# Fetching the next expert's weights in parts, one to two batches ahead, with their quarter sums one at a time between accumulating transfers

## The chip, the cores and the metric

The kernel runs on one core of a Trainium2 chip. The metric is device time in microseconds (us), lower is better. A kernel is run several times, beside runs of the kernel before on the same chip. A ratio is the mean time of one kernel's fast runs over that of the other's fast runs of the same rounds, so it is not quite the ratio of the medians that are quoted. PE is TensorE, ACT is ScalarE, DVE is VectorE, and POOL is GpSimd, which also issues most of this kernel's DMA (76.8 of 94.33 MB, worked out from the issues on the page of before).

## The reference, cut to what matters

Attention with a hash mask produces 3072 tokens of 512 numbers. They then pass through eight experts, each of them two matrices with a ReLU between, weighted by a routing matrix `P`:

```python
B, H, S, D = 4, 8, 768, 64            # 3072 tokens in 4 batches of 768
for e in range(8):
    h = np.maximum(x @ w1[e], 0.0)    # 512 x 1024
    ye = h @ w2[e]                    # 1024 x 512
    out += P[:, e:e + 1] * ye
```

Experts 1 to 7, four batches each, take about two thirds of the time.

## The kernel before

Each product of experts 1 to 7 is computed from 2 x 2 blocks with seven block products instead of eight. This needs sums and differences of the blocks of both operands. The four sums of each weight matrix ("quarter sums") are made on POOL. The four sums of the hidden activations h are made on DVE for each of the three steps of a batch:

```python
wpool = ctx.enter_context(tc.tile_pool(name="wpool", bufs=2))
...
def quarters_of_w(e):
    if (e, 1) not in weights:
        load_w(e, 1, pin=True)              # one 1 MB transfer (f32 to f16), issued by POOL
    ...
    pin(nc.gpsimd.tensor_tensor(s[:, 0], a21, a22, op=Alu.add))
    pin(nc.gpsimd.tensor_tensor(a21, a11, a21, op=Alu.subtract))
    pin(nc.gpsimd.tensor_tensor(s[:, 1], s[:, 0], a11, op=Alu.subtract))
    pin(nc.gpsimd.tensor_tensor(s[:, 2], a12, s[:, 1], op=Alu.subtract))
    ...
# quarters_of_w2(e) does the same for w2

def sums_of_h(e, b, i):                     # on DVE, both inputs in SBUF
    ...
    pin(nc.vector.tensor_tensor(s_[:, 0], h21, h22, op=Alu.add))             # s1
    pin(nc.vector.tensor_tensor(s_[:, 1], s_[:, 0], h11, op=Alu.subtract))   # s2
    pin(nc.vector.tensor_tensor(h21, h11, h21, op=Alu.subtract))             # s3
    pin(nc.vector.tensor_tensor(s_[:, 2], h12, s_[:, 1], op=Alu.subtract))   # s4
```

`pin` keeps an instruction in program order. `hidden(e, b)` makes the h of a batch. `mixed(e, b)` multiplies it by w2 in three steps i = 0, 1, 2. PE alternates between `hidden` of one batch and `mixed` of the batch before it (`woven`). In every step ACT copies four partial results from PSUM into a buffer `vt`, and POOL issues a transfer that adds `vt` to the result `acc`:

```python
def mixed(e, b):
    for i in range(J // 2):
        ...
        vt = vkeep.tile([P, 4, DD // 2], F32, tag="v", name="vt")      # vkeep: bufs=3
        ...                                                            # seven products; ACT fills vt
            if g == 3 and i + 1 < J // 2:
                sums_of_h(e, b, i + 1)
            if g == 6:
                if not last:
                    pin(nc.gpsimd.dma_start(out=acc[:, b, i], in_=vt, accum_op=Alu.add))
...
ORDERS = (("a1", "d", "a2", "y", "a3", "a4", "t"), ...)    # step 0: a2 reads s2, y reads s3, a4 reads s4
...
hspool = ctx.enter_context(tc.tile_pool(name="hspool", bufs=3))
vkeep = ctx.enter_context(tc.tile_pool(name="vkeep", bufs=3))
...
def hidden(e, b):
    if b == 2 and e < E - 1:
        quarters_of_w(e + 1)
    if b == 3 and e < E - 1:
        quarters_of_w2(e + 1)
...
def woven(n):
    h = hidden(*work[n]) ...
    c = mixed(*work[n - 1]) ...
        sums_of_h(*work[n - 1], 0)          # the first DVE sums of a batch: right at its start
```

The softmax here doesn't subtract the row's maximum and nothing guards it: scores larger than these inputs give would overflow.

## Time and profile before

Before takes 915.38 us (median of 3 runs, 914.61 to 917.09).

| expert stage of the kernel before | us | where it is read |
|---|---|---|
| one undisturbed batch | 18.46 | spacing of the accumulating transfers at the end of the run |
| four undisturbed batches | 73.9 | worked out: 4 x 18.46 |
| from expert to expert, mean | 89.3 | spacing of the first weight load of each |
| POOL waits for weights | 127.3 | view of waits: 66.6 + 60.7 |
| ACT waits for a free vt | 66.5 | view of waits |

First a stretch without weight work, from the table of windows. Its columns are start and end, length, then busy time and number of instructions of PE, PE's weight loads, DVE, ACT and POOL, then PE's granted clock, the DMA share, and GB/s. PE is busy for 64.49 of 65.00 us at full clock, so PE is the bound wherever nothing stops it.

```profile
800.00:865.00 65.00, 64.49 (x490) 47.63 (x489) 49.64 (x116) 41.55 (x97) 9.29 (x11) 1.00 0.57 117
```

The view of waits has who waited for whom, then us in total, times, and the longest. These are the lines of the loop that stops PE:

```profile
POOL t L147 <- DMA t<-in_moe_w_dram: 66.6, 5, 13.6
ACT vt L208 <- DMA acc<-vt: 66.5, 12, 7.2
...
PE a L201 <- ACT vt L208: 62.4, 17, 6.4
...
POOL s L134 <- DMA t<-in_moe_w_dram: 60.7, 6, 10.6
```

POOL's timeline around one such place follows (start, duration, line, operation; in brackets the idle time before it and what ended it). The load goes out at 558.00, POOL sits for 10.60 us, then runs four sums of about 2.1 us. The accumulating transfers that came due meanwhile go out three in a row (x3) at 578.30. The same happens for w2 until 604.75 (this one wait, of 14.27 us, the view puts down to PE; the other five of L147 it puts down to the load).

```profile
557.47 0.84 POOL L246 DMA_DIRECT2D acc<-vt  x1 [4.60 <-ACT hT L664]
558.00 1.09 POOL L113 DMA_DIRECT2D t<-in_moe_w_dram  x1
569.70 2.12 POOL L134 TENSOR_TENSOR s<-t 128x1024 f16<-128x1024 f16 x1 [10.60 <-DMA t<-in_moe_w_dram]
...
578.30 2.57 POOL L246 DMA_DIRECT2D acc<-vt  x3
579.97 1.84 POOL L113 DMA_DIRECT2D t<-in_moe_w_dram  x1
596.08 2.12 POOL L147 TENSOR_TENSOR t<-t 128x1024 f16<-128x1024 f16 x1 [14.27 <-PE y L201]
...
604.75 2.62 POOL L246 DMA_DIRECT2D acc<-vt  x3
```

PE's timeline at the same place: it stops for 6.40 us, because ACT has no free vt, and then the four matmuls of a group take 1.01 us in place of 0.60. The windows view gives a granted clock of 0.52 from 583.8 to 588.6.

```profile
575.69 0.60 PE L201 MATMUL a<-t,hT 128*128 128x256 f16 x4
...
583.80 1.01 PE L201 MATMUL a<-t,hs 128*128 128x256 f16 x4 [6.40 <-ACT vt L208]
```

POOL sums also meet the DVE sums of h (L176 to L179, usually 0.42 us each) in this trace: 17 of the DVE sums last 0.77 to 2.38 us. Eleven fall within 2 us before one of the stalls on vt, where a delay can't be told from the stall. Two of the rest are shown. At 506 us the last DVE sum, s4, is held up, and PE loses 0.23 us. At 774 us three POOL sums in a row hold up three DVE sums, s2, s3 and s4, and PE loses 4.10 us. What PE waits for last, both times, is the DVE operation L215 (it adds a product to `acc`), which comes after them:

```profile
506.00 0.42 DVE L178 TENSOR_TENSOR hT<-hT 128x512 f16<-128x512 f16 x1
506.02 2.38 POOL L147 TENSOR_TENSOR t<-t 128x1024 f16<-128x1024 f16 x1 [13.20 <-DMA t<-in_moe_w_dram]
506.33 2.35 DVE L179 TENSOR_TENSOR hs<-hT,hs 128x512 f16<-128x512 f16 x1
...
509.99 0.60 PE L201 MATMUL y<-t,hT 128*128 128x256 f16 x4 [0.23 <-DVE acc L215]
...
774.74 2.12 POOL L147 TENSOR_TENSOR t<-t 128x1024 f16<-128x1024 f16 x1 [13.32 <-DMA t<-in_moe_w_dram]
774.76 2.38 DVE L177 TENSOR_TENSOR hs<-hs,hT 128x512 f16<-128x512 f16 x1
...
777.06 2.34 DVE L178 TENSOR_TENSOR hT<-hT 128x512 f16<-128x512 f16 x1
...
779.32 2.33 DVE L179 TENSOR_TENSOR hs<-hT,hs 128x512 f16<-128x512 f16 x1
...
782.96 1.00 PE L201 MATMUL y<-t,hT 128*128 128x256 f16 x4 [4.10 <-DVE acc L215]
```

### The profile page before, as it was taken

What the parts mean: (1) busy time and instruction counts of PE and PEld (TensorE: products, weight loads), DVE (VectorE), ACT (ScalarE), POOL (GpSimd) and SP (SyncE); (2) the same over time, 40 slices, a digit from 0 to 9 for tenths busy, and PEclk for the clock granted to TensorE, in tenths of its full rate; (3) what the DMA queues carried; (4) which work ended last, traced back from release to release, by engine and by line L of the source; (5) the groups of instructions that cost most, each with busy time, mean ns of one, the idle gap of its engine ahead of it and who ended that gap; (6) DMA issues with size and microseconds to landing.
All of it is one profiled execution on the core that took longest, in us unless ns stands there. A gap on an engine that the chain in (4) does not pass through costs nothing.

```text
span 916.0 us, 16844 instructions
## 1 busy us (share of the span) xinstructions
PE 781.9 (85%) x6412; PEld 536.5 (59%) x6412; DVE 560.0 (61%) x1213; ACT 516.7 (56%) x1033; POOL 300.0 (33%) x311
## 2 busy tenths in 40 slices
PE   4789999998999789978997899779977997899830
PEld 1456666565556557755775577457755775577620
DVE  2335656454658766766775677557765776777710
ACT  1767677776457567644664466446644664466510
POOL 6545443491001541154115412441244134311110
PEclk9879999999999899989998999889998998999965
DMA  6965576410004555555366445634564456447653
GB/s 190 243 155 155 139 182 131 127 40 1 1 1 86 92 94 99 102 92 102 74 116 105 80 92 93 115 70 92 93 116 82 81 93 116 93 79 149 141 119 89
DMA packets 44720, 94.33 MB, mean 103 GB/s; under 512 B 10656, under 2 KB 23968, under 8 KB 44640
## 3 DMA queue, kind: packets, MB, share of 16 engines
q0 software_dynamic: 29920, 77.88, 44.5%
q1 hardware_dynamic: 13920, 14.77, 5.9%
q8 instruction: 50, 0.82, 0.4%
q10 hardware_dynamic: 800, 0.62, 0.3%
q14 instruction: 30, 0.25, 0.1%
HBM read 53.14 MB, written 7.08 MB: 66 GB/s over the span
## 4 chain that ended last, share of the span: by engine, by line
PE 52%; DMA 23%; POOL 7%; issue 6%; ACT 5%; DVE 4%; SPq 1%; POOLq 0%; ACTq 0%; DVEq 0%
PE a L201 10%; PE a L625 10%; DMA t<-in_moe_w_dram 9%; DMA acc<-vt 8%; PE d L625 7%; PE y L201 5%; PE st L418 5%; PE hp L476 3%; PE num L434 2%; PE yp L159 2%; ACT pt L421 2%; PE yp L486 2%; PE d L201 2%; POOL t L135 1%; POOL s L136 1%
## 5 line engine op out<-in xcount | busy, mean ns | idle before, releaser
L208 ACT ACTIVATE vt<-a,p 128x256 f32<-128x256 f32 x335 | 158.5, 473 | 233.5 <-PE a L201 167.0
L634 DVE CUSTOM_DVE_ANT_0 hT<-d,u 128x384 f16<-128x384 f32 x336 | 185.1, 553 | 168.9 <-ACT u L630 163.8
L201 PE MATMUL a<-t,hs 128*128 128x256 f16 x1008 | 162.3, 287 | 63.5 <-ACT vt L208 62.4
L421 ACT ACTIVATE pt<-st 128x768 f16<-128x768 f32 x192 | 147.2, 809 | 72.9 <-PE st L418 72.1
L246 POOL DMA_DIRECT2D acc<-vt x83 | 71.0, 972 | 333.6 <-ACT vt L208 119.9
L630 ACT COPY u<-a 128x384 f32<-128x384 f32 x336 | 160.7, 478 | 32.7 <-PE a L625 24.2
L201 PEld LDWEIGHTS <-hT 128*128 128x128 f16 x1344 | 134.1, 100 | 61.1 <-issue 9.6
L201 PEld LDWEIGHTS <-hs 128*128 128x128 f16 x1008 | 102.7, 102 | 107.5 <-issue 58.0
L625 PE MATMUL a<-xT,s 128*128 128x384 f16 x448 | 116.4, 343 | 0.1
L418 PE MATMUL st<-qs,ks 71*128 71x384 f16 x384 | 98.1, 338 | 17.4 <-DMA qs<-ds 13.2
L625 PEld LDWEIGHTS <-t 128*128 128x128 f16 x896 | 89.2, 100 | 39.4 <-issue 4.8
L201 PE MATMUL y<-t,hT 128*128 128x256 f16 x672 | 106.6, 284 | 5.1 <-DVE acc L215 5.0
L625 PE MATMUL d<-xd,t 128*128 128x384 f16 x448 | 109.8, 327 | 0.0
L215 DVE SCALAR_TENSOR_TENSOR acc<-y,p,acc 128x256 f32<-128x256 f32 x168 | 80.3, 478 | 17.2 <-PE y L201 17.1
L434 PEld LDWEIGHTS <-pt 128*128 128x128 f16 x1152 | 62.5, 99 | 28.5 <-issue 3.9
L625 PEld LDWEIGHTS <-s 128*128 128x128 f16 x672 | 67.8, 101 | 19.4 <-issue 2.3
L434 PE MATMUL num<-va,pt 128*128 128x65 f16 x1152 | 68.4, 196 | 0.6 <-ACT pt L421 0.6
L625 PE MATMUL a<-xT,t 128*128 128x384 f16 x224 | 57.2, 338 | 0.0
L625 PE MATMUL d<-xT,t 128*128 128x384 f16 x224 | 56.3, 334 | 0.0
L330 POOL CAST t<-acc 128x768 f16<-128x768 f32 x32 | 26.3, 825 | 90.6 <-DVE acc L329 90.3
L418 PEld LDWEIGHTS <-ks 71*128 71x128 f16 x384 | 33.4, 100 | 38.5 <-issue 13.1
L664 ACT ACTIVATE hT<-a 128x384 f16<-128x384 f32 x112 | 54.1, 483 | 2.9 <-PE a L625 2.9
(94 smaller groups left out, 961.8 us busy)
## 6 DMA issues: line engine op xcount, KB each, us to landing
acc<-vt POOLq DMA_DIRECT2D x83, 512.0 KB, 5.1
t<-in_moe_w_dram POOLq DMA_DIRECT2D x16, 1024.0 KB, 11.2
acc<-in_k_dram POOLq DMA_DIRECT2D x7, 768.0 KB, 5.7
acc<-in_q_dram POOLq DMA_DIRECT2D x7, 768.0 KB, 6.0
v<-in_v_dram POOLq DMA_DIRECT2D x28, 192.0 KB, 4.5
out_dram<-acc SPq DMA_DIRECT2D x18, 256.0 KB
ks<-t SPq DMA_DIRECT2D x64, 48.0 KB
qs<-t SPq DMA_DIRECT2D x56, 48.0 KB
```

The source lines that it names most:

```text
L201: pin(nc.tensor.matmul(dst, hq[hn][:, fo, :], wq[wn][:, fo, :], start=first and fo == 0, stop=fo == FH - 1, skip_group_check=True))
L208: pin(nc.scalar.activation(out=vt[:, k], in_=a, func=Act.Copy, scale=p))
L215: pin(nc.vector.scalar_tensor_tensor(out=dst, in0=src, scalar=p, in1=dst, op0=Alu.mult, op1=Alu.add))
L246: pin(nc.gpsimd.dma_start(out=acc[:, b, i], in_=vt, accum_op=Alu.add))
L418: pin(nc.tensor.matmul(st[:, i, 0:HT], d["k"][0:KR, h, kt * P:(kt + 1) * P], d["q"][0:KR, h, i * HT:(i + 1) * HT], start=True, stop=True))
L421: pin(nc.scalar.activation(out=pt, in_=st[:, :, 0:HT], func=Act.Exp, scale=scale))
L434: pin(nc.tensor.matmul(num[:, j * (D + 1):(j + 1) * (D + 1)], pf[:, j * P:(j + 1) * P], va[:, h, kt, :], start=(kt == 0 and j == 0), stop= ...
L476: pin(nc.tensor.matmul(hp[:, 0:HT], w1[:, do, fo * P:(fo + 1) * P], xT[:, do, b * S + t * HT:b * S + (t + 1) * HT], start=(do == 0), stop= ...
L625: pin(nc.tensor.matmul(bk, wq[wn][:, do, f * P:(f + 1) * P], xq[xn][:, do, :], start=first and do == 0, stop=do == 1, skip_group_check=True))
L630: pin(nc.scalar.copy(t, bk))
L634: pin(add(TENSOR_ADD_SAT, out=dst, in0=bk, in1=u, s0=3e38, s1=0.0))
L664: pin(nc.scalar.activation(out=hT[:, f, hi], in_=a, func=Act.Relu))
```

## The change

The intent is that POOL should never sit waiting for weights. Loads are cut into halves and issued well ahead. At the end of every step (`next(coming)`, after the accumulating transfer) POOL gets one half load or one quarter sum, or nothing. There are three steps per batch, so twelve such places ("slots") per expert. Slots 1, 2, 4 and 5 load. Slots 6 to 13 sum, where 13 is also slot 1 of the expert after and gets a sum and a load. Slots 6, 9 and 12 are ends of batches. One hs buffer is given up and one vt buffer is added.

```diff
-    def load_w(e, which, pin=False):
+    def load_w(e, which, pin=False, half=None):
...
+        part = slice(0, t.shape[1]) if half is None else slice(half * t.shape[1] // 2, (half + 1) * t.shape[1] // 2)
+        ins = nc.gpsimd.dma_start(out=t[:, part], in_=src[:, part])
...
         pin(nc.gpsimd.tensor_tensor(s[:, 0], a21, a22, op=Alu.add))
+        yield
         pin(nc.gpsimd.tensor_tensor(a21, a11, a21, op=Alu.subtract))
+        yield
...                                          # likewise after the other sums, and in quarters_of_w2
+    def next_weights():
+        for e in range(2, E):
+            for which in (1, 2):
+                for half in range(2):
+                    load_w(e, which, pin=True, half=half)
+                    yield
+                if which == 1:
+                    yield
+            for g in (quarters_of_w(e), quarters_of_w2(e)):
+                for n in range(4):
+                    next(g, None)
+                    if g.__name__ == "quarters_of_w" or n < 3:
+                        yield
+        while True:
+            yield
+    coming = next_weights()
...                                          # mixed, end of each step, after the accumulating transfer
+                    next(coming)
...
-    hspool = ctx.enter_context(tc.tile_pool(name="hspool", bufs=3))
-    vkeep = ctx.enter_context(tc.tile_pool(name="vkeep", bufs=3))
+    hspool = ctx.enter_context(tc.tile_pool(name="hspool", bufs=2))
+    vkeep = ctx.enter_context(tc.tile_pool(name="vkeep", bufs=4))
...                                          # hidden
-        if b == 2 and e < E - 1:
-            quarters_of_w(e + 1)
-        if b == 3 and e < E - 1:
-            quarters_of_w2(e + 1)
...                                          # woven
+        if n == 0:
+            for _ in range(3):
+                next(coming)
```

More of the change, by code (lines that the diff above doesn't have):

```diff
@@ L104 @@
     weights = {}
-    def load_w(e, which, pin=False):
-        if which == 1:
+    def load_w(e, which, pin=False, half=None):
+        if half == 1:
+            t = weights[e, which]
+            src = (moe_w1[e].rearrange("(do di) f -> di do f", di=P) if which == 1
+                   else moe_w2[e].rearrange("(fo fi) d -> fi fo d", fi=P))
+        elif which == 1:
             t = wpool.tile([P, DO, F], F16, tag="w1")
@@ L112, in load_w @@
             src = moe_w2[e].rearrange("(fo fi) d -> fi fo d", fi=P)
-        ins = nc.gpsimd.dma_start(out=t, in_=src)
+        part = slice(0, t.shape[1]) if half is None else slice(half * t.shape[1] // 2, (half + 1) * t.shape[1] // 2)
+        ins = nc.gpsimd.dma_start(out=t[:, part], in_=src[:, part])
         if pin:
@@ L147, in quarters_of_w2 @@
         pin(nc.gpsimd.tensor_tensor(t[:, 1], b22, b12, op=Alu.subtract))
+        yield
         pin(nc.gpsimd.tensor_tensor(b12, b12, b11, op=Alu.subtract))
+        yield
         pin(nc.gpsimd.tensor_tensor(t[:, 0], b22, b12, op=Alu.subtract))
+        yield
         pin(nc.gpsimd.tensor_tensor(t[:, 2], b21, t[:, 0], op=Alu.subtract))
         weights[e, "t"] = dict(b11=b11, t1=b12, b21=b21, b22=b22, t2=t[:, 0], t3=t[:, 1], t4=t[:, 2])
+    def next_weights():
[3 more added lines that the diff above has]
+                    load_w(e, which, pin=True, half=half)
+                    yield
+                if which == 1:
+                    yield
+            for g in (quarters_of_w(e), quarters_of_w2(e)):
+                for n in range(4):
+                    next(g, None)
+                    if g.__name__ == "quarters_of_w" or n < 3:
+                        yield
+        while True:
+            yield
+    coming = next_weights()
     def combine(b):
@@ L525 @@
             if n == len(groups) - 1 and i == 2:
-                quarters_of_w(1)
-                quarters_of_w2(1)
+                for _ in quarters_of_w(1):
+                    pass
+                for _ in quarters_of_w2(1):
+                    pass
             if u + 1 < len(units):
```

## The prediction

Three passages that rest on no trace of this case are cut from the recorded text where marked. Its sum came to 915.4 - 93 + 5 = 827 us. The 93 is worked out from the trace of before, the 5 is an estimate from the two meetings in it.

> **What bounds the kernel now.** After about 260 us the expert stage is bound by TensorE: undisturbed, PE is busy 64.5 of 65.0 us (table of windows, 800 to 865 us, clock 1.00), and one batch takes 18.46 us (every third accumulating transfer in the timeline of POOL). Four batches are 73.9 us, but experts follow each other every 88.4 to 91.7 us, 89.3 on average (first weight load of each). So 15.4 us per expert is lost, some 93 us over six transitions.
>
> **Where it goes.** POOL's timeline shows one queue doing all: it issues a whole 1 MB weight load, sits 10 to 14 us until it lands (view of waits: 66.6 us for w2, 60.7 us for w1), then runs four sums of 2.12 us. The accumulating transfers acc<-vt due meanwhile stand behind this; three go out together afterwards (578.30, 604.75). With three vt buffers ScalarE then waits for one (66.5 us, 12 times), and TensorE for ScalarE: twelve stalls of 4.0 to 6.4 us, 62 us together, two per expert. After each the matmul groups last 1.01 us in place of 0.60 for some 4.5 us, about 2.3 us more per stall, 27 us together. [...] gaps of 0.5 us leave 0.60. 62 + 27 = 89 us, close to 93.
>
> **What the change does.** Same bytes, same eight sums. Loads go out in halves at the ends of steps, at least four steps (about 24 us) before the first sum that reads them, so POOL should never sit on one. Between two accumulating transfers stands at most one sum (2.1 us) or one half load's issue (about 1 us), with 6.15 us from step to step. A fourth vt buffer gives a transfer about 18 us to land; alone it takes 5.1, and behind a half load (estimated 5.6, half of the whole's 11.2) some 11. The third hs buffer isn't needed: its last reader is a step old when it is rewritten.
>
> **New cost.** The sums now run beside full-speed compute. The DVE sums of h (two SBUF inputs, 0.42 us) sometimes take 2.27 us beside a POOL sum[...]. Three of eight sums per expert fall at a batch's end, where the next DVE sums are due. In the trace such a collision cost TensorE 0.23 us, once 4.1 us. I allow 0.2 to 0.5 us for each of some 20 collisions: 4 to 10 us. Attention, routing and the 51 us tail stay.
>
> **Predicted:** 915.4 - 93 + 5 = 827 us; 816 to 845 should hold it 8 times in 10. Faster by over 2%: 0.96; within 2%: 0.03; slower: 0.01.
>
> **What would show it.** POOL's waits for weight loads vanish; ScalarE's wait for acc<-vt falls from 66.5 us to under 5; no 1.01 us matmul groups between 265 and 860 us; experts every 74 to 76 us. DVE sums of over 2 us grow in number, with PE waits under 1 us on DVE. Landing of acc<-vt rises (maximum about 12 us) but nobody waits.
>
> **What would make it wrong.** Collisions might idle TensorE long enough to drop its clock; two half loads in succession might delay acc<-vt beyond four buffers[...]. Each would leave it at 840 to 870.

## The result, and the profile after

The changed kernel takes 869.96 us (median of 4 runs, 868.53 to 874.65) against 916.24 us (4 runs, 914.61 to 918.03). The ratio of the fast runs is 0.9503, with a 95% interval of 0.946 to 0.9547. That is 5% faster, but above the predicted range of 816 to 845.

In the view of waits the loop of before is gone. POOL waits for no weight load any more, and ACT waits for no accumulating transfer. A new pair stands in its place: PE, and PE's weight loads, wait 18 times for the DVE sum on L207, which is s2 (17 of them, of 1.6 to 2.4 us, at the end of a batch whose slot has a sum; the last is 0.5 us at the end of the run).

```profile
PEld L231 <- DVE hs L207: 39.8, 18, 2.8
...
PE a L231 <- DVE hs L207: 33.1, 18, 2.4
```

POOL's timeline shows the plan at work: single loads and single sums between the transfers, with no waiting for weights. From 594.83 to 613.28, with no sum at the batch's end, a batch takes 18.45 us, as long as an undisturbed one of before.

```profile
588.44 0.85 POOL L276 DMA_DIRECT2D acc<-vt  x1 [5.71 <-ACT vt L238]
589.04 2.40 POOL L161 TENSOR_TENSOR t<-t 128x1024 f16<-128x1024 f16 x1
591.12 1.01 POOL L118 DMA_DIRECT2D t<-in_moe_w_dram  x1
594.83 0.86 POOL L276 DMA_DIRECT2D acc<-vt  x1 [2.71 <-ACT hT L693]
...
613.28 0.83 POOL L276 DMA_DIRECT2D acc<-vt  x1 [4.49 <-ACT hT L693]
...
619.32 2.41 POOL L139 TENSOR_TENSOR s<-t 128x1024 f16<-128x1024 f16 x1
```

The next batch, with the sum at 619.32 at its end, has its second transfers at 613.28 and 633.82 us: 20.54 us. So a sum at a batch's end costs 2.1 us. The timeline of all engines at such a place shows how. The transfer goes out at 559.21, just as the DVE sums of the next batch begin. The POOL sum follows at 559.81 and ends at 562.20. The DVE sum s2, started at 559.50, lasts 2.99 us instead of 0.42 and ends at 562.49. The first PE product that reads s2 starts then, after 1.89 us of idling.

```profile
559.05 0.42 DVE L206 TENSOR_TENSOR hs<-hT 128x512 f16<-128x512 f16 x1
559.21 0.85 POOL L276 DMA_DIRECT2D acc<-vt  x1 [2.43 <-ACT hT L693]
...
559.50 2.99 DVE L207 TENSOR_TENSOR hs<-hs,hT 128x512 f16<-128x512 f16 x1
...
559.81 2.39 POOL L145 TENSOR_TENSOR s<-t,s 128x1024 f16<-128x1024 f16 x1
...
562.42 0.41 DVE L208 TENSOR_TENSOR hT<-hT 128x512 f16<-128x512 f16 x1
...
562.55 0.61 PE L231 MATMUL a<-t,hs 128*128 128x256 f16 x4 [1.89 <-DVE hs L207]
```

The account runs over the same 26 batches in both traces, from the first accumulating transfer of all to the first one of the second-last batch. Before needs 851.4 - 278.8 = 572.6 us and after 805.8 - 280.1 = 525.7 us. Undisturbed they would need 484.0: 3 batches of the first expert at 19.8 us (the spacing of its matmul groups in the trace of before, 278.29 to 298.08) and 23 of 18.46. So before lost 88.6 us there and after loses 41.7 us. The old stalls are gone, and nearly half of their worth was given back to the new wait.

### The profile page after: what moved, and what is told of

It is laid out like the page before. It is cut to its first block, busy times and chain, and to the rows that moved or that the text cites. A ratio compares the mean times of both kernels' runs of the same rounds, so it can differ in the third digit from the quotient of the medians.

```text
span 866.8 us, 16857 instructions
## 1 busy us (share of the span) xinstructions
PE 763.8 (88%) x6412; PEld 526.9 (61%) x6412; DVE 583.7 (67%) x1213; ACT 514.9 (59%) x1033; POOL 308.0 (36%) x323
## 4 chain that ended last, share of the span: by engine, by line
PE 68%; DVE 13%; ACT 7%; DMA 5%; issue 2%; POOL 1%; SPq 0%; ACTq 0%; POOLq 0%
PE a L231 14%; PE a L654 14%; PE d L654 9%; PE y L231 7%; PE st L449 6%; DVE hs L207 6%; ACT pt L452 4%; DVE hT L663 4%; PE hp L507 4%; PE num L465 3%; DMA acc<-vt 3%; PE yp L517 2%; PE yp L189 2%; PE d L231 2%; DVE acc L245 2%
## 5 line engine op out<-in xcount | busy, mean ns | idle before, releaser
L231 PE MATMUL a<-t,hs 128*128 128x256 f16 x1008 | 153.2, 275 | 35.9 <-DVE hs L207 33.1
L231 PEld LDWEIGHTS <-hT 128*128 128x128 f16 x1344 | 131.3, 98 | 53.8 <-issue 2.0
L231 PEld LDWEIGHTS <-hs 128*128 128x128 f16 x1008 | 97.8, 99 | 78.1 <-DVE hs L207 39.8
L654 PE MATMUL a<-xT,s 128*128 128x384 f16 x448 | 111.2, 330 | 0.1
L231 PE MATMUL y<-t,hT 128*128 128x256 f16 x672 | 101.8, 274 | 1.7 <-DVE hT L208 1.1
L207 DVE TENSOR_TENSOR hs<-hs,hT 128x512 f16<-128x512 f16 x84 | 79.4, 946 | 2.9
L654 PEld LDWEIGHTS <-s 128*128 128x128 f16 x672 | 66.0, 98 | 17.8 <-issue 2.3
L654 PE MATMUL a<-xT,t 128*128 128x384 f16 x224 | 55.2, 328 | 0.0
```

The costliest lines, as they stand in the source:

```text
L231: pin(nc.tensor.matmul(dst, hq[hn][:, fo, :], wq[wn][:, fo, :], start=first and fo == 0, stop=fo == FH - 1, skip_group_check=True))
L654: pin(nc.tensor.matmul(bk, wq[wn][:, do, f * P:(f + 1) * P], xq[xn][:, do, :], start=first and do == 0, stop=do == 1, skip_group_check=True))
```

## The experiments

The theory after the result: the 42 us are lost where a POOL sum runs at the same time as the first DVE sums of a batch. Four rivals were tested. The first is that a POOL sum costs its time wherever it stands. The second is that a batch's end is dear for another reason. The third is that each meeting has a fixed price. The fourth is that half loads or late transfers cause the loss. A separate question is which part of the change earned the gain.

For most of the experiments the generator was replaced by one with two tables, so that only a table differs from run to run:

```python
LOADS = {1: (1, 0), 2: (1, 1), 4: (2, 0), 5: (2, 1)}     # slot: (matrix, half), as in the change
SUMS = {6: 1, 7: 1, 8: 1, 9: 1, 10: 1, 11: 1, 12: 1, 13: 1}   # slot: number of sums, as in the change

def next_weights():
    todo = {e: eight_sums(e) for e in range(2, E)}        # the sums of w1, then of w2, one per next()
    slot = 0
    while True:
        slot += 1
        for e in range(2, E):
            for _ in range(SUMS.get(slot - 12 * (e - 2), 0)):
                next(todo[e])
        for e in range(2, E):
            if slot - 12 * (e - 2) in LOADS:
                which, half = LOADS[slot - 12 * (e - 2)]
                load_w(e, which, pin=True, half=half)
        yield
```

| run | what it is | median us | ratio to before (95%) |
|---|---|---|---|
| the change | | 869.96 | 0.9503 (0.946 to 0.9547) |
| a1_off_ends | no sum at a batch's end | 836.35 | 0.9118 (0.9073 to 0.9163) |
| f1_no_sums | no sums at all for experts 2 to 7 (wrong result) | 831.65 | 0.907 (0.9014 to 0.9127) |
| c1_before_4vt | before, with the change's buffers only | 872.31 | 0.9515 (0.947 to 0.956) |
| d1_after_3vt | the change, with before's buffers | 868.89 | 0.9434 (0.9359 to 0.9509) |
| g1_pause | the change, batch-end sums about 1.5 us later | 838.52 | 0.9153 (0.9109 to 0.9197) |
| h1_half_sums | half a sum at a batch's end | 849.9 | 0.927 (0.9221 to 0.9319) |
| i1_off_ends_3vt | a1 with before's buffers | 830.89 | 0.9075 (0.9023 to 0.9127) |
| j1_off_ends_whole | a1 with whole loads | 834.31 | 0.9107 (0.9062 to 0.9152) |
| b2_early_only | early whole loads, sums in fours at batch ends, before's buffers | 902.1 | 0.9835 (0.9756 to 0.9915) |

All are medians of four runs and gave correct results, except f1. Its output is wrong, which doesn't matter for the time. The runs were made on three chips, each beside its own runs of before, so they are compared by their ratios. One run of d1, the profiled one, fell in the slow state. Its ratio uses the other three (858.47 to 869.0), and its trace is not used.

### Sums moved off the ends of batches (a1_off_ends)

```diff
-    SUMS = {6: 1, 7: 1, 8: 1, 9: 1, 10: 1, 11: 1, 12: 1, 13: 1}
+    SUMS = {4: 1, 5: 1, 7: 1, 8: 1, 10: 1, 11: 1, 13: 1, 14: 1}
```

> Same loads, same eight sums, but one sum at the end of the first and of the second step of a batch and none at a batch's end. Theory (the lost time sits where a POOL sum meets the first DVE sums of the next batch): the 18 TensorE waits of about 1.9 us for the DVE sum s2 vanish, a batch takes 18.46 us throughout, 828 to 834 us. Rival (a POOL sum costs about 2 us of DVE time wherever it stands): no better than 865 us.

Measured: 836.35 us. The same eight sums and the same loads, moved by a step or so, take about 34 us less. No s2 sum in the trace is longer than 0.43 us (the line below is from the view of tile hs; after the count come the least, median and greatest duration in ns, then the first and last start). Of the waits of PE for it, one of 0.5 us is left at the end of the run.

```profile
L213 DVE TENSOR_TENSOR hs<-hs,hT x84: 424/425/426, 270.9 to 785.3; 128x512 f16<-128x512 f16 x84
```

So a sum does not cost its time wherever it stands, and the first rival falls. The result is 2 us above the expected range. In the trace PE still waits 1.37 and 1.28 us for the DVE in the first expert, where DVE also makes the block sums of x. Four of these take 2.65 to 2.94 us beside a POOL sum, where the others take 0.55.

### No sums at all (f1_no_sums)

```diff
         s = spool.tile([P, 3, 2, F // 2], F16, tag="s1")
+        (for e > 1: raw quarters take the place of the sums, no POOL operation; the same for w2)
```

> The changed kernel with the sums of experts 2 to 7 taken away (raw quarters in their place: wrong result on purpose). Theory: the same as without sums at batch ends, 826 to 832 us, since the other sums cost nothing. Rival (something else, such as the half loads or the landing of transfers, makes the 2 us): stays at 860 us or more.

Measured: 831.65 us, with half loads and transfers as in the change. Its interval overlaps those of a1 and i1, so sums away from the ends of batches cost nothing that these times can tell from noise. The traces tell a little more. By the account over 26 batches a1 still loses 767.2 - 279.0 - 484.0 = 4.3 us, most of it in the first expert, and f1 loses 0.4, against the 41.7 of the change. The half loads and the landing of transfers do not make the 42 us, and the fourth rival falls.

### Only the buffers (c1_before_4vt), and all but the buffers (d1_after_3vt)

```diff
 c1: before, with          hspool bufs=3 -> 2, vkeep bufs=3 -> 4
 d1: the change, with      hspool bufs=2 -> 3, vkeep bufs=4 -> 3
```

> The kernel before with only the buffers of the change: vt 4, hs 2. A stall of 4.0 to 6.4 us ends when one more transfer has landed, and a fourth buffer gives 5.4 to 6.6 us more. If the buffer is the larger part of the gain, 840 to 870 us. If the early fetch and spreading are what counts, 900 us or more.

> The changed kernel with the buffers of before: vt 3, hs 3. With POOL never blocked a transfer has 12 us to land. If early fetch and spreading are what counts, 868 to 876 us. If the fourth buffer is, 890 us or more with ScalarE waiting for acc<-vt behind the half loads.

Measured: 872.31 us, 2 us above the range that was expected if the buffer counts, and 868.89 us, in the range expected if the early fetch does. I had not seen this coming when I predicted: one more vt buffer alone, with POOL still sitting on whole loads, earns what the whole change earns. The rescheduling alone, without the buffer, earns it as well. The two are substitutes. That each removes the stall on vt is seen in the trace of c1; for d1 it is inferred, from its time and from i1 below, which has the same three buffers. In c1's view of waits POOL still waits for the weights, but ACT hardly waits for transfers. PE now waits for the DVE sums here as well, because the eight POOL sums, no longer hidden in a stall, run beside them (at 491 to 497 us DVE sums of 1.57, 2.22 and 2.33 us beside POOL sums of 2.12 to 2.18):

```profile
POOL s L134 <- DMA t<-in_moe_w_dram: 60.4, 6, 10.6
...
PE a L201 <- DVE hs L177: 19.1, 12, 3.0
...
PE y L201 <- DVE hT L178: 6.3, 6, 1.3
ACT vt L208 <- DMA acc<-vt: 5.4, 5, 1.5
```

### The batch-end sum a little later (g1_pause)

```diff
+                    if slot % 3 == 0:                                 # a batch's end
+                        pin(nc.gpsimd.memset(pauses[0], 0.0))         # 128 x 640 f16
+                        pin(nc.gpsimd.memset(pauses[0], 0.0))
                     next(todo[e])
```

> The changed kernel's order of sums; only each of the 18 batch-end sums stands behind two write-only fills on POOL (about 1.25 us, estimated from the 0.195 us of a 128-wide and 1.39 us of a 1560-wide fill). Theory (what costs is the overlap in time with the four DVE sums of h, which last some 1.7 us): the sum starts when they are over, and 18 x 2.07 us come back: 830 to 842 us, s2 at 0.42 us. Rival (a sum at a batch end is dear for another reason, e.g. it holds up the transfer behind it): 868 us or more, as POOL has more to do.

Measured: 838.52 us, though POOL has more to do. The sum stands at the same slot, behind the same transfer and in the same order, but starts 2.1 us after that transfer instead of 0.6. The DVE sums are over by then. Thus a batch's end is dear only for the overlap in time, and the second rival falls. The trace also shows that the fills, which only write, run beside the DVE sums (L218 to L220) without lengthening them. A DVE sum that meets the POOL sum, the next step's at 523.90, is lengthened to 0.87 us, but has time to spare.

```profile
520.50 0.43 DVE L218 TENSOR_TENSOR hs<-hs,hT 128x512 f16<-128x512 f16 x1
520.76 0.94 POOL L183 MEMSET pause<- 128x640 f16 x1
520.84 0.42 DVE L219 TENSOR_TENSOR hT<-hT 128x512 f16<-128x512 f16 x1
521.18 0.42 DVE L220 TENSOR_TENSOR hs<-hT,hs 128x512 f16<-128x512 f16 x1
...
522.36 2.13 POOL L139 TENSOR_TENSOR s<-t 128x1024 f16<-128x1024 f16 x1
523.90 0.87 DVE L217 TENSOR_TENSOR hs<-hT 128x512 f16<-128x512 f16 x1
```

### Half a sum at the batch's end (h1_half_sums)

```diff
-        pin(nc.gpsimd.tensor_tensor(s[:, 0], a21, a22, op=Alu.add))
+        hsum(s[:, 0], a21, a22, Alu.add, 0)      # first half of the columns
+        yield
+        hsum(s[:, 0], a21, a22, Alu.add, 1)      # second half
+    SUMS = {6: 1, 7: 1, 8: 2, 9: 1, 10: 1, 11: 4, 12: 1, 13: 1, 14: 4}     # counted in halves
```

> Still 18 POOL operations at batch ends, but each is half a sum (512 of 1024 columns); the other half goes at the next step's end. Theory (TensorE waits as long as the POOL operation that hit s2): the wait falls from 1.9 to about 0.8 us, 848 to 856 us. Rival (a fixed price per meeting): 868 us.

Measured: 849.9 us, about half of the loss. The typical PE wait for s2 falls from 1.89 to 0.91 us, and the waits come to 17.7 us in total against 33.1.

```profile
526.28 2.02 DVE L233 TENSOR_TENSOR hs<-hs,hT 128x512 f16<-128x512 f16 x1
526.56 1.45 POOL L133 TENSOR_TENSOR s<-t 128x512 f16<-128x512 f16 x1
...
528.36 0.61 PE L257 MATMUL a<-t,hs 128*128 128x256 f16 x4 [0.92 <-DVE hs L233]
```

The third rival, a fixed price per meeting, falls. The wait follows the length of the POOL operation, less some 0.5 us both times: 2.39 and 1.89 us with a whole sum, 1.45 and 0.92 with a half.

### Which parts of the change the better schedule needs (i1_off_ends_3vt, j1_off_ends_whole)

```diff
 i1: a1, with  hspool bufs=2 -> 3, vkeep bufs=4 -> 3
 j1: a1, with  LOADS = {1: (1, None), 4: (2, None)}      # whole matrices
```

> The schedule with no sum at a batch's end, with vt 3 and hs 3 as before. Theory (the fourth buffer only absorbs a blocked POOL, and nothing blocks it here): 833 to 840 us, as with vt 4. Rival (the fourth buffer is needed behind the half loads): 845 us or more.

> The schedule with no sum at a batch's end, with each matrix loaded by one 1 MB transfer instead of two halves. If cutting the loads matters, acc<-vt lands too late behind 11 us of load and ScalarE waits: over 842 us. If not (four vt buffers give 18 us), 833 to 840 us.

Measured: 830.89 and 834.31 us. With the sums off the batch ends neither the fourth buffer nor the cutting into halves is needed: i1 and j1 are not slower than a1, and i1 lies 2 us below its expected range. In i1, ACT waits for an accumulating transfer once, for 1.4 us. i1 is faster than both kernels, and its interval (0.9023 to 0.9127) lies clear of the change's. Its time can't be told from that of f1, so little is left to gain from the POOL sums.

### Only the early fetch (b2_early_only)

```diff
 a1, with  SUMS = {9: 4, 12: 4}, whole loads in slots 1 and 4, hspool bufs=3, vkeep bufs=3
```

> Of the change only the early fetch: whole loads, issued at least four steps ahead, buffers as before (vt 3, hs 3), the sums four in a row at two batch ends per expert. Theory: POOL is held up for at most 8.8 us, so three vt buffers do, ScalarE waits under 10 us for acc<-vt, but the first two sums of each four meet the DVE sums, some 3 us each of 12 times: 865 to 880 us, a third way to the same gain as the buffer alone and as the change. Rival (the spreading is what freed the transfers): ScalarE keeps waiting for acc<-vt, 885 us or more.

Measured: 902.1 us, well above what I expected; at a ratio of 0.9835 it is faster than before, but not clearly by 2%. Half of the expectation held: ACT waits only 2.3 us in all for accumulating transfers, with three buffers and four sums in a row. The other half was too mild. I had put a group of four at 3 us. The trace has waits of 1.87, 1.32, 1.02 and 0.86 us in one group, 5.1 us together, since each POOL sum holds up the next DVE sum in turn:

```profile
508.83 2.98 DVE L213 TENSOR_TENSOR hs<-hs,hT 128x512 f16<-128x512 f16 x1
509.10 2.42 POOL L155 TENSOR_TENSOR t<-t 128x1024 f16<-128x1024 f16 x1
511.60 2.19 POOL L157 TENSOR_TENSOR t<-t 128x1024 f16<-128x1024 f16 x1
511.73 2.33 DVE L214 TENSOR_TENSOR hT<-hT 128x512 f16<-128x512 f16 x1
511.87 0.61 PE L237 MATMUL a<-t,hs 128*128 128x256 f16 x4 [1.87 <-DVE hs L213]
```

So the early fetch alone frees the transfers but returns most of that to meetings with the DVE. Where the sums fall decides the time: 902 us with all eight at batch ends, 870 with three of eight, and 831 to 836 with none.

## Why the prediction was wrong

- **The bound and its loss: right.** I predicted some 93 us lost in the expert stage. The account over 26 batches gives 88.6. What did not come is its full return: experts follow each other every 80.1 us in the changed kernel (first sums at 539.26 and 619.32), where I had said 74 to 76.
- **The loop of POOL, vt and PE: right.** POOL's waits for weights and ACT's waits for acc<-vt vanish. Of the twelve stalls, though, only eleven belong to it: the one of 4.10 us at 774 us, counted among them, is the meeting with the DVE sums. The slow matmul groups are gone from twelve places, but not from all: after three of the new waits (1.94, 2.42 and 2.09 us, near 296, 320 and 743 us) single groups of 1.06 us show up for some 3 us. The granted clock is 0.72, 0.76 and 0.76 over the 6 to 7 us around them (windows 294 to 300, 318 to 325 and 741 to 748). After the others the groups last 0.61. In the trace of before the slow groups followed stalls of 4.0 to 6.4 us; these three followed shorter waits.
- **What earns it: only partly seen.** I counted early loads, halves, spreading and the buffer as one. The buffer alone gives 872 us, the rest without it 869, and the halves make no difference (j1). An estimate in the same text was off without effect: a half load takes 8.2 us to land (median of the 24 on the page of the changed kernel), where I had put 5.6.
- **The step that failed: "I allow 0.2 to 0.5 us for each of some 20 collisions: 4 to 10 us".** The number of meetings was right (18), and their place too ("three of eight sums per expert fall at a batch's end"), but each costs 2.1 us of batch length, of which 1.9 us is PE idling; in the first expert, where DVE has more to do, three batches take 1.5 to 4.9 us more than their 19.8. The new cost was 41.7 us over the 26 batches, not 5. With this term, 827 - 5 + 41.7 = 864 us, within 1% of the result (a check of the sum with the measured cost, not a new prediction). The prediction had named collisions that idle PE as a risk that would leave it at 840 to 870; the idling came, the drop of the clock after only three.
- **Why it was mis-sized.** The trace of before held two prices, 0.23 and 4.10 us, and I took the lower as the rule. Neither is that of the new place. Both meetings stood in the middle of a batch, where the DVE sums are made a step ahead; PE lost only what L215, behind one held-up sum or three, came too late. In the changed program the POOL sum starts 0.6 us after the transfer of the batch's last step, while s2 is under way, and here PE waits for s2 itself, which the third product of the batch's first step reads. It held up s2 17 times of 18, and once s3 (at 421 us, with a PE wait of 1.13 us). The program order fixes that place, so the meeting should have been counted as certain, and its price as the length of the POOL operation less a slack of some 0.5 us (h1). The lengthening itself is plain in the traces: 0.42 becomes 2.99 us beside a POOL sum (the changed kernel), and stays 0.42 to 0.43 beside a fill (g1).

## What to carry to other kernels

When work is moved out of a stall, price it at the new place, against the instruction that it will meet there and the slack of whoever reads that one's result, and not at the mildest meeting in the old trace. If one engine's operation lengthens another's (here 0.42 to 2.99 us), try the movable one a step away: here the same sums cost some 34 us more at one place than a step or so away. Before believing that a schedule earned a gain, try the buffer count that came with it by itself.

## What these runs leave open

- By the profile's times the DVE sum s2 started 0.31 us before the POOL sum (559.50 and 559.81), yet it ended about 0.3 us after it, at 2.99 us instead of 0.42. The POOL sum took 2.39 us, no longer than the 2.40 of one away from a batch's end. Why the one that started first is the one held up, no run here settles.
- Waits of 1.94, 2.09 and 2.42 us in the changed kernel were followed by groups of 1.06 us, and one of 1.99 us in c1_before_4vt by groups of 1.03 us at a granted clock of 0.52 (495 to 500 us). Waits of 1.87 to 1.91 us in the changed kernel left 0.61, and so did one of 2.19 us in c1_before_4vt for the group right after it (the next one, after 1.14 us more of waiting, took 1.03). What decides between them is open.
- How the price of such a meeting follows from who reads the held-up result, and when, was measured at few places: 0.23 us for an s4 made a step ahead and 1.9 us for an s2 that is read at once, with a POOL sum of the same length (2.38 and 2.39 us).
